# 32-bit attention products on 64 stationary columns, one query load per tile, and a new order

## The chip, the cores and the metric

The kernel runs on one core of a Trainium2 chip. The metric is the device time of one execution in microseconds (us), the median of several runs. TensorE (PE) multiplies, VectorE (DVE), ScalarE (ACT) and GpSimd (POOL) do the rest, and all DMAs are issued by SyncE (SP), whose queue is in order.

## The reference

Four batches of 768 positions go through an attention of eight heads (64 wide) and then a feed-forward layer of width 512 to 2048 to 512. A position attends to its window of 15 neighbours on both sides and to 24 block summaries (the maximum of 32 keys, the mean of 32 values):

```python
k_sum = k.reshape(B, H, nb, block, D).max(axis=3)
v_sum = v.reshape(B, H, nb, block, D).mean(axis=3)
scores_l = scale * np.matmul(q, k.transpose(0, 1, 3, 2))      # only |i - j| < 16 is kept
scores_s = scale * np.einsum('bhsd,bhnd->bhsn', q, k_sum) + np.log(block)
a = softmax(concatenate([masked scores_l, scores_s]))
x = np.matmul(a, np.concatenate([v, v_sum], axis=2))          # heads side by side: B x S x 512
xn = (x - mean) / sqrt(var + 1e-6) * g_ln
out = x + np.maximum(xn @ w_ch1, 0.0) @ w_ch2
```

## The kernel before

Positions are cut into 24 tiles T of 128, six per batch; two halves of four heads make 48 units t = 2T + hh.

**The first batch** (t = 0 to 11) is computed in 32 bits. `early_qk(t)` makes the scores: per unit two halves of the array's rows (`pr`, contraction over 64) and two heads (`v`), four matmuls with 128 stationary columns (the queries). `early_transp` transposes the probabilities against an identity (tiles `pp`), and `early_pv(t, pr)` multiplies them with the values into a tile `o`: one matmul of 128 columns on the common tail and two of 64 on the near values, again with 128 stationary columns, contraction over 128. In the first four units spare transposes of `ident` stand ahead of them.

**The other three batches** are computed with pairs of 16-bit numbers. `load_q` fetches queries into `qs` twice (one copy for each half of the partitions) and splits them, `heads(T)` makes scores and products with 64 stationary columns, the two halves of the output's partitions by turns, `late_softmax` follows. Before a batch starts, `batch(b)` passes its keys, queries and values through one staging tile (`bst`, one buffer) to find block sums and the largest magnitudes: each load is followed by an Abs with a sum on ACT, after which the next load may start. `batch_vput` writes the block means (`vsum`) into the value tiles by eight small DMAs per batch.

**The feed-forward layer** runs through all of it as the filling of PE. `g1(s)` makes a piece of the hidden layer (tile `h`, two buffers in PSUM), evicted by a Relu on ACT and a subtraction on DVE; `g2(s)` multiplies it into the outputs (tile `a`). Weights are merged, measured (`gram`) and split first.

**The order** on each engine is not that of the code. Every call is recorded in `Plan`, with a cost per instruction, and `Plan.issue` simulates all engines and writes the instructions out in the simulated order of their starts. The table `ORDER` shifts the rank of every step:

```python
early = 16.0 * np.frombuffer(base64.b85decode(ORDER), "<i4")
rank, best = [r + early[x.stage] for r, x in zip(rank, self.ops)], None
```

Each engine then runs its list strictly in order. A helper (line 356, after the change line 361) issues all of it, so the profile gives one line for everything and groups are told apart by tiles. DMA costs in `MOVE` are by partitions and bytes: time in the shared queue and tail; one number `ISSUE` or `TURN` is the issuing time on SP.

Of the kernel before, what the change touches and what calls it, by code (L numbers as in the profile page):

```python
# [34 lines left out]
NE = 192  # L35
# [24 lines left out]
    "nCAcgSgHU2Q#t?uV$A>l)BXSdK@<Q0=`;WU>qh_p4_E*I+0+03N8JDa9k>7g#GwEGn+X5_f13aQ$;to!&{O~bqq+b8UhV(?0doKVZ`l9;lm7qz"  # L60
    "Sk(Xj56S=k?JfWSl1cyowH5#X1^oa2e>wmF=EVR1?-"
    "u|7#@+w_(~<xG8w~&e1|t9fLr?$!W=jA7jcfn_5P1Lq5uE@3nLq#l=UM;&+}{8H9R&aYvj6}8v2p+azx@CIp#}f|WVrwTcA5YG=N|w7r=|b@Nk"
    "0Gp1ik<NJCy(bap3>|TCo5BUC#giIr;zpC6539A;JIusmTBTO%wnCpUwaO1q%QGS?T}(UI_pI!}kCGKh^*Ln;rlFxVHcQ>l6S0%@hCt)bIcQ5e"
    "EPOSqlIF`&s}1>0kf=1^EB}E4csvfS~{X+3ElPstN!A&C37(cjy2Ay^H_<$IAczzn%a8PMrV$Dq#Qs54`{XfY<;3?YsZ~jQ0Qkrv?B3IpF{QjO"
    "PFU$F2YW!T<mN;Kl#{xTydC6XpN^CK~_%!t?+CW8VM&m?QuIdKUlyG`;`-"
    "TgU(ZJ0t)ARZjo_R^k8u7^MII$F~3f>H`1(wkH4pD_j5ooCN>?CJq1q*NOlCI{E+q(!&4$JKF#MS<3(asmuTWix&U@^4S0XI<x=(c%=XTq80!E"
    "1dRXx_x1n(6<PoQ!1(|FlZ*fVR@(pnU>pDdArt@rJvsmY15^M2S3m#&(JBA{YbyW%3v2)YrYZmcWdZ;I1aJTVNiF~YKX?EDNBjT(2<`v>L|Xs="
    "Tp<7eHaP$QnX&)>;4c6G-a7yQX(a#v82|tOinIU!ZV><gB+dW-+@1gb9q<4Dz1{!+_DBE#EhPW|txNy_sLKEUKm-"
    "5)%&GtXdBp$!4!r;W8Uz3UBgFszR{#J1&gTFB@7(|YU=08OMz#O{PwM~w3L^jjyD<O&QWyXLEFJ&=&o2M~GHL(-#>oHw>|p=^B-"
    "a1`LgxSf=S2Vj1qlEEUjYCBAx;1Qdp-aFS{ncWU?%_o{0{&Cwm1L)2>t*6*2n+<#sB~REc*Zdvj6}9vp@g<Nk{+yjvD{~c-"  # L70
    "a5{Wf1@Xwr2nUur>eya!UXJUPk}`zHI;i>uvx50(t-djvD{~{!0J=Jsto6BtifH2U-9Cv`_#5w?+T}H6{Q6F+>0W7w-"
    "T6RyqIxI~o80flvSd&L02($}j)`e?0&I)c^nh3NHWvuo(aV+T{QL)baoSF24W&?=}DcIqm=d!twwA6S)8XGBp4I<6i&(vGM=^{^I}tQ1Ac$kk$"
    "YH1vmfzvcdoVRrde?$pQcX??C_naV!7;03QGV7100xg;M|k-"
    "v<By?JWQR1vCHvoX`LNnNI)!Qwab7c%T3OUG4w>L<Rr=(<%S}n9%?K3NruzoGbtUx=8>4U)=xyFaQ7mAHe_r*9-"
    "svyVw8!GNS+gDiZ(zDy{$j_ZI*FHv<3wzzP5Ww($S|T<ib;=)V8|BryO0OWXhdJ{SN1qVE6yMf?B%&msT-CqV!J2T1?`^-"
# [16 lines left out]
    "}!Kr;XUxhDVs-tYhak}d!M!@mFj3zPr<#JvCip&I}I16%+ADB1u29<u-cVUGX*6qEn|$5j9T!_@!(T)+SSVJiRttg8S2`1k++fx-"
    "X(Ru}*PCv^Y-L0<p>mMs7Ppwj>U94!C<A;SOvMyvn-Bs~BC88ZL?!NLFkyIcSO2Q&Zxeq8_ndKUlyD`)@!;#>d#K{5aU4jljhY#aapHB<lqv2g"
    "$Z=?nk>p+W!v$2b50HEsX^!%YAHekA|^rV;=EMF;=@<01e6Yb5{xo6i6LZ43YahB5#EpHct-"
    "4*387f<gcQaHaqM3&#Kdui^jyL0<p>dm{h<(7XTt73}~2AkqK-O1%I7RsjG2tS<lnAVvTHwe$b~eeD1Lk{<v7mZ|^$"
# [11 lines left out]
class Plan:  # L107
# [8 lines left out]
    MOVE = {
        "T": (1520.0, 550.0),
        (1, 2048): (170.0, 880.0),
        (128, 1024): (610.0, 490.0),
        (128, 1536): (680.0, 790.0),  # L120
        (128, 2048): (750.0, 880.0),
        (128, 2944): (1530.0, 960.0),
        (128, 3072): (1360.0, 1010.0),
        (128, 4096): (1770.0, 1290.0),
        (128, 576): (40.0, 2010.0),
        (24, 512): (110.0, 730.0),
        (32, 1024): (40.0, 820.0),
        (32, 2048): (40.0, 2000.0),
        (64, 1024): (220.0, 830.0),
        (64, 2048): (750.0, 770.0),  # L130
        (96, 1024): (490.0, 590.0),
        (96, 2048): (800.0, 700.0),
# [1036 lines left out]
```

## Time and profile before

| | |
|---|---|
| median of 2 runs | 632.82 us (631.36 to 634.27) |
| the profiled execution | 631.18 us, its span 629.4 us |
| PE busy | 616.1 us, 98% |
| DVE, ACT, POOL busy | 401.6, 351.1, 147.0 us |
| granted TensorE clock, mean | 0.995 |
| DMA | 89.52 MB, mean 142 GB/s |

A row of the page's groups reads: line, engine, operation, out<-in with shapes, count, then busy time and mean duration, then the idle time of the engine before it and what ended it. A row of a timeline begins with the start and the time that the row covers; ends of matmuls are modelled, so the pace of PE is read from starts. A row of stretches gives, for a stretch of time, its length and the busy time of PE, weight loads, DVE, ACT and POOL, then the granted clock, the DMA share and GB/s. One execution is profiled; sums are made against its own time.

### The profile page before, as it was taken

The numbers are of one execution on the slowest core, as the hardware profiler recorded it, in microseconds if no ns is written. First come the engines' busy times: TensorE is split into PE (matmuls) and PEld (weight loads), VectorE is DVE, ScalarE is ACT, GpSimd is POOL, SyncE is SP. The second block draws the span as 40 slices with busy tenths as digits, with TensorE's granted clock in tenths as the row PEclk, the third lists the DMA queues.
The fourth block names the chain that finished last, engine by engine and source line by source line (L and its number), as shares of the span: only waits on it lengthen the run. The fifth ranks groups of instructions, "written<-read, shape, count | busy, mean of one in ns | idle before, by whom it ended". The sixth has DMA issues, their size and how long they took to land.

```text
span 629.4 us, 14009 instructions
## 1 busy us (share of the span) xinstructions
PE 616.1 (98%) x5227; PEld 427.5 (68%) x5227; DVE 401.6 (64%) x1098; ACT 351.1 (56%) x926; POOL 147.0 (23%) x271
## 2 busy tenths in 40 slices
PE   8999999999999999999799999999999999999997
PEld 6777779885544676667377884577766756677754
DVE  4899999879668268846687465676877821171211
ACT  4898985459977257746677364565767711121100
POOL 4110302201333005403343022441433410030000
PEclk9999999999999999999799999999999999999999
DMA  9968798454797627555976426835776350011001
GB/s 285 308 175 259 237 302 231 99 159 120 192 226 166 151 73 191 155 159 134 199 209 139 95 70 125 188 83 146 176 152 151 74 120 0 1 48 23 1 25 43
DMA packets 115831, 89.52 MB, mean 142 GB/s; under 512 B 69553, under 2 KB 100273, under 8 KB 115762
## 3 DMA queue, kind: packets, MB, share of 16 engines
q1 hardware_dynamic: 115762, 88.61, 54.9%
q8 instruction: 41, 0.67, 0.4%
q14 instruction: 28, 0.23, 0.1%
HBM read 66.27 MB, written 6.29 MB: 115 GB/s over the span
## 4 chain that ended last, share of the span: by engine, by line
PE 60%; DMA 14%; ACT 10%; DVE 9%; SPq 4%; issue 2%; POOL 0%; ACTq 0%; DVEq 0%; POOLq 0%
PE h L356 26%; PE a L356 24%; SPq L356 4%; DMA bst<-in_ks 3%; DMA qs<-in_qt 3%; DMA bst<-in_vs 3%; PE o L356 3%; PE s L356 3%; DMA bst<-in_qa 2%; ACT p L356 2%; DVE m L356 2%; ACT bst L356 2%; PE low L356 1%; ACT w L356 1%; DVE kmax L356 1%
## 5 line engine op out<-in xcount | busy, mean ns | idle before, releaser
L356 PE MATMUL h<-xt,w_u 128*128 128x256 f16 x2304 | 264.5, 273 | 2.2 <-DVE h_x L356 2.2
L356 PEld LDWEIGHTS <-w_u 128*128 128x128 f16 x2304 | 224.8, 98 | 39.0 <-issue 5.0
L356 PE MATMUL a<-w,h_x 128*128 128x512 f16 (+1 forms) x960 | 211.8, 376 | 4.5 <-ACT h_x L356 4.1
L356 PEld LDWEIGHTS <-h_x 128*128 128x128 f16 x1008 | 98.0, 98 | 107.6 <-ACT h_x L356 5.1
L356 DVE SCALAR_TENSOR_TENSOR h_x<-h,h_x 128x512 f16<-128x512 f32 x80 | 54.1, 685 | 88.4 <-ACT h_x L356 88.3
L356 ACT ACTIVATE h_x<-h 128x512 f16<-128x512 f32 x80 | 46.2, 590 | 96.1 <-PE h L356 95.9
L356 ACT ACTIVATE p<-p,mn,sv 128x120 f32<-128x120 f32 x144 | 68.2, 475 | 12.6 <-POOL mn L356 12.3
L356 ACT ACTIVATE bst<-bst 128x384 f32<-128x384 f32 (+2 forms) x55 | 32.4, 589 | 52.3 <-DVE vsum L356 25.5
L356 POOL TENSOR_TENSOR p<-p,p 128x480 f16<-128x480 f32 x36 | 40.8, 1134 | 63.1 <-ACT p L356 52.4
L356 POOL TENSOR_TENSOR x<-x,rc 128x256 f32<-128x256 f32 x36 | 28.2, 789 | 94.5 <-DVE x L356 91.5
L356 PE MATMUL a<-w,h_y 128*128 128x512 f16 x192 | 43.6, 379 | 0.0
L356 POOL TENSOR_SCALAR mn<-mn,sv 128x4 f32<-128x4 f32 x36 | 19.2, 534 | 99.5 <-DVE mn L356 80.0
L356 DVE SCALAR_TENSOR_TENSOR m<-raw,m 128x512 uint32<-128x512 uint32 x64 | 42.1, 680 | 0.0
L356 DVE SCALAR_TENSOR_TENSOR qhl<-qs,sv,qhl 64x512 f16<-64x512 f32 x36 | 28.4, 788 | 18.9 <-ACT qhl L356 18.1
L356 DVE CUSTOM_DVE_ANT_0 p<-s,mask 128x120 f32<-128x120 f32 x144 | 33.4, 275 | 7.6 <-PE s L356 7.4
L356 ACT ACTIVATE qhl<-qs,sv 128x512 f16<-128x512 f32 x36 | 25.7, 714 | 19.8 <-DMA qs<-in_qt 14.8
L356 DVE SCALAR_TENSOR_TENSOR kl<-ksg,sv,kh 128x640 f16<-128x640 f32 x36 | 32.1, 891 | 7.3 <-ACT kh L356 6.9
L356 DVE SCALAR_TENSOR_TENSOR x<-a,scales,x 128x512 f32<-128x512 f32 (+1 forms) x24 | 17.7, 735 | 27.7 <-PE a L356 27.5
L356 ACT ACTIVATE kh<-ksg,sv 128x640 f16<-128x640 f32 x36 | 29.5, 821 | 6.9 <-DMA ksg<-in_kt 5.8
L356 PEld LDWEIGHTS <-h_y 128*128 128x128 f16 x192 | 18.7, 98 | 21.0
L356 DVE TENSOR_REDUCE x<-o 128x256 f32<-128x512 f32 x36 | 23.8, 684 | 9.1 <-PE o L356 9.1
L356 DVE SCALAR_TENSOR_TENSOR v<-vst,sv,v 128x512 f16<-128x512 f32 x36 | 29.2, 821 | 0.0
(116 smaller groups left out, 722.3 us busy)
## 6 DMA issues: line engine op xcount, KB each, us to landing
raw<-in_w SPq DMA_DIRECT2D x32, 512.0 KB
ksg<-in_kt SPq DMA_DIRECT2D x36, 368.0 KB
qs<-in_qt SPq DMA_DIRECT2D x72, 128.0 KB
out_x<-x SPq DMA_DIRECT2D x23, 256.0 KB
bst<-in_ks SPq DMA_DIRECT2D x20, 192.0 KB
bst<-in_qa SPq DMA_DIRECT2D x15, 256.0 KB
bst<-in_vs SPq DMA_DIRECT2D x20, 192.0 KB
vst<-in_va SPq DMA_DIRECT2D x36, 96.0 KB
```

Of the source, the lines that this page charges most:

```text
L356: getattr(getattr(nc, self.ops[i].engine), op)(*a, **k)
```

## The change

Four things change. In `early_qk` and `early_pv` each 32-bit matmul is issued twice, for the two halves `z` of the stationary columns, which write the two halves of the output's partitions. The planner's cost of such a half is half of the whole. The queries are loaded by one DMA that writes both halves. Issuing time in `MOVE` becomes a third number for each kind of DMA, all three numbers of every kind are new, and `ORDER` is a new table (its text is left out here).

```diff
-        "T": (1520.0, 550.0),
+        "T": (1320.0, 1450.0, 790.0),
...
-    ISSUE, TURN, BEGIN, TICK, SWITCH, FIRST = 470, 1250, 1100, 10240 / 3, 93, 3500
+    BEGIN, TICK, SWITCH, FIRST = 1100, 10240 / 3, 93, 3500
...
-        (128, 2048): (750.0, 880.0),
+        (128, 2048): (420.0, 850.0, 1060.0),
...
-        (24, 512): (110.0, 730.0),
+        (24, 512): (790.0, 100.0, 860.0),
...
-        for half in range(2):
-            nc.sync.dma_start(qs[D * half : D * half + D], qt[T, hh])
+        nc.sync.dma_start(qs[:], qt[T, hh].partition_broadcast(2))
...
-                    nc.tensor.matmul(ps[pr][:, v * NE : v * NE + w], q[:, v], k[:, v, :w], start=True, stop=True)
+                    for z in halves:
+                        nc.tensor.matmul(
+                            ps[pr][z, v * NE : v * NE + w], q[:, v, z], k[:, v, :w], start=True, stop=True
+                        )
...
-            nc.tensor.matmul(both, e[:, 1, :], tail, start=True, stop=False)
+            for z in halves:
+                nc.tensor.matmul(both[z], e[:, 1, z], tail, start=True, stop=False)
             for v in range(2):
                 j = 2 * v + pr
-                nc.tensor.matmul(ps[:, j, :], e[:, 2 * v, :], near[:, j], start=False, stop=v == 1)
+                for z in halves:
+                    nc.tensor.matmul(ps[z, j, :], e[:, 2 * v, z], near[:, j], start=False, stop=v == 1)
```

What the change moves is shown at three places. The first is PE early in the program, the PV products of unit 1 (tile `o_124`; `pT` are the transposed probabilities, `vst` and `spare_x` the values) and the scores of unit 4 (`s_..._160` and `161`). Before:

```order
L356 MATMUL s_0_160<-spare_x_100,spare_x_94 128x184
L356 MATMUL s_1_161<-spare_x_100,spare_x_94 128x184
L356 MATMUL s_0_160<-spare_x_100,spare_x_94 128x192
L356 MATMUL s_1_161<-spare_x_100,spare_x_94 128x192
L356 MATMUL o_124<-ident 128x128
L356 MATMUL o_124<-vst_77,pT_0_123 128x2x64
```

And now:

```order
L361 MATMUL o_124<-ident 128x128
L361 MATMUL o_124<-vst_77,pT_1_126 64x2x64 x2
L361 MATMUL o_124<-spare_x_96,pT_1_126 64x64 x4
L361 MATMUL s_0_160<-spare_x_100,spare_x_94 64x184 x2
L361 MATMUL s_1_161<-spare_x_100,spare_x_94 64x184 x2
L361 MATMUL s_0_160<-spare_x_100,spare_x_94 64x192 x2
L361 MATMUL s_1_161<-spare_x_100,spare_x_94 64x192 x2
L361 MATMUL pp_0_149<-ident,p_88 128x128 x3
```

Every row of the first batch's products stands for two matmuls on 64 partitions each, and the PV products no longer have the array shape of the transposes around them. Over the whole program PE's list has 12 runs of QK and 20 of the 64-column products of the later batches between full-array work before, and 12 of QK, 20 of the later batches and 21 of PV now. Four of the 21 border on a run of QK on one side; after 11 of them comes a 32-bit instruction of the full array.

The second place is ACT in the middle of the program, where queries of the fourth batch pass through `bst` (`bst92` and `bst93`, sums to `vabs3`) while tile 14 is attended to; `h38` and `h40` are hidden pieces with their Relu, `kh`, `qhl`, `v16` the split operands. Before:

```order
L356 ACTIVATE bst92_775,vabs3_761<-bst92_775 128x512
L356 ACTIVATE kh0_379<-ksg28_703,sv2_581 128x4x160
L356 ACTIVATE qhl28_702<-qs74_701,sv2_581 128x512
L356 ACTIVATE v16_0_378<-vst0_77,sv2_581 128x8x64
L356 ACTIVATE v16_1_382<-vst1_78,sv2_581 128x8x64
L356 ACTIVATE bst93_776,vabs3_761<-bst93_776 128x512
L356 ACTIVATE h38_x3_639<-h38_638 128x512
```

And now:

```order
L361 ACTIVATE h38_x3_639<-h38_638 128x512
L361 ACTIVATE bst91_774,vabs3_761<-bst91_774 128x512
L361 ACTIVATE h38_x3_639<-h39_640 128x512
L361 ACTIVATE p_87,sum26_684<-p_87,mn26_683,sv2_581 128x120 x3
L361 ACTIVATE p2_88,sum27_686<-p2_88,mn27_685,sv2_581 128x120
L361 CAST p16_376<-p_87 128x4x120
L361 ACTIVATE p2_88,sum27_686<-p2_88,mn27_685,sv2_581 128x120 x2
L361 ACTIVATE bst92_775,vabs3_761<-bst92_775 128x512
L361 ACTIVATE p2_88,sum27_686<-p2_88,mn27_685,sv2_581 128x120
L361 CAST p16_376<-p2_88 128x4x120
L361 ACTIVATE bst93_776,vabs3_761<-bst93_776 128x512
L361 ACTIVATE h40_x4_688<-h40_687 128x512
```

The Abs of `bst93` has moved from before the Relu of `h38` to before that of `h40`. On PE, 54 matmuls of `a` stand between the products of `h38` and those of `h40` now, and then the 24 of `h41`. On SP, in the same stretch, the loads of `bst92` and `bst93` now stand like this (`ksg` are keys, `pt` transposed probabilities; the last of the eight copies of `vsum2` stands 13 rows ahead of the first row, before the load of `bst89`):

```order
L361 DMA bst92_775<-in_qa 128x512
L361 DMA vst1_78<-in_va 64x256
L361 DMA qs77_724<-in_qt 128x1x512
L361 DMA vst1_78<-in_vb 32x256
L361 DMA vst1_78<-in_va 96x256
L361 DMA ksg30_726<-in_kt 128x2x368
L361 DMA_TRANSPOSE pt1_381<-p16_376 128x8x128
L361 DMA bst93_776<-in_qa 128x512
```

Before, six of the eight copies, two transposes and the two query loads stood between the two:

```order
L356 DMA bst92_775<-in_qa 128x512
L356 DMA qs74_701<-in_qt 64x512
L356 DMA vst0_77<-vsum2_569 24x128 x2
L356 DMA vst1_78<-vsum2_569 24x128
L356 DMA_TRANSPOSE pt0_377<-p16_376 128x8x128
L356 DMA vst1_78<-vsum2_569 24x128
L356 DMA qs74_701<-in_qt 64x512
L356 DMA vst1_78<-vsum2_569 24x128 x2
L356 DMA_TRANSPOSE pt0_377<-p16_376 128x8x128
L356 DMA bst93_776<-in_qa 128x512
```

The copies and the loads of this unit's queries have left the stretch between the two; loads of values and a transpose of the next tile stand there.

The third place is PE where the second batch's magnitudes are brought together (`vps1`). Before, products for the weights' size (`gram2`, of the merged weights `m2`) and of `h15` stand around it:

```order
L356 LDWEIGHTS m2_1_330
L356 MATMUL gram2_0_359<-m2_1_330 128x128
L356 MATMUL vps1_440<-ident_76,vm0_1_439 3x128
L356 LDWEIGHTS w1_u14_323
L356 MATMUL h15_412<-xt_1_186,w1_u14_323 128x256
```

And now products of `a0`:

```order
L361 LDWEIGHTS h0_y0_386
L361 MATMUL a0_1_388<-w2_3_363,h0_y0_386 128x512
L361 MATMUL vps1_440<-ident_76,vm0_1_439 3x128
L361 LDWEIGHTS h2_y1_391
L361 MATMUL a0_0_387<-w2_4_364,h2_y1_391 128x512
```

The output products of the first two tiles have moved ahead of the second batch's first scores; before, they began after them.

More of the change, by code (lines that the diff above doesn't have):

```diff
@@ L60 @@
[L60 to L75, printed above, removed]
@@ L92 @@
[L92 to L95, printed above, removed]
+    "QSJZ#i{t<QdmR7(uHgUw&#wRfvEBdw8@m7hbEN<O60QIL*{}cq$Or%c?%V(W4v_!<=-"
+    "2=M8TSAGExiB#Z?pgZ3q$|_Sr7mK@eBX}8;$?}KfnL~kJ|tLxm5rFG5Y`iSw#Q<y_x_28t4E2Z6E*u?5Y3%-"
@@ new lines @@
+    "k|^gx$yu04AcMrdX@kG<hlR<UHSk2`9S~xL>d49+r<C>thN9DU<CjGkJA7D^=SYA&Mg1{&msT-"
+    "2DJbGmWu!X;`#so4K@G(7|s9x2*&^a6P^G6;=lj@vi<-"
+    "6$EW}Q!N~vrJCXnY?3VxkBennk>5c#YfT;ifmD~USu8aTwp^N|jhPMCz*P;Lalmq|(UWWhw55)if`jP+tg5m%F4Tt~#ET{kf8IS+}n4kauYsLT"
+    "nyd(esaUK8w+Svd96Ab_W*T(<<CHnvW3XuQ*<In&9M)3dt`P2XZXx{(-"
+    "<mLbWqs0IJE$09Kg+TxSB+UQ+F}nZ%1RekYD{24$&JX|q^0fc|t;7HSag+c53>p9c0`UL;wlV+!y9EFMUm*Yh2}J+^C@ug1TH*iy@w)&2JfHvn"
+    "&Cvh<c=iAPMWp}#tLOj!L{0zzqo)7=2l4;^G+qDzg0uhsEjR!G!rTA<F5dtD{xbjo>1zN02Q&Zx02%-Q0cijL$0`5-"
@@ new lines @@
+    "sWJcn3j+WEhr<8=pD6$U;4uII%vk^c0$>0DeQW>#x>5iD)9?TPUt$0NGHU<;8p{9w_5=U`7zF?T)pP&=kR1R3h5P^iU&;Uf&$<8qtS<lnQ;h%r"
+    "|7-"
+    "vNbG85fT$2C)eCGfEJeB|ddZqvWNd5o+?uGyVf3pAoXW0M$wEqA9W(EKN7t#O!eB1y3t@r=`78L*h=;HtXqZ$AJ>$d;@;sO8wu<ZZ;&kq0qas&"
+    "VXpdSDL>2&}AYgPaNvEcvz?UVoip`ic&?eYKrSqcCEN3H+=;@<!Nf06(H6u|%gtiJ#M*^~eOa7zFH$kYG-BBB5P+pPcpuL}SGOcVeBgt7nsE7t"
+    "%2UXK6&vKIgVUDyBr%9{WGKJEYi4JZHrQUw42BLDyZmsS7(BVhmlLJt4{Iw}AFwkQAqb3Fh6kRt#9k^cYxE*}5@yA}Wd=2-"
+    "v$V{`xjn)3huLmmJCVW<E9(f0rUufYHRN)7-3pz;6z2-"
@@ new lines @@
+    "hr$cpU%$y&M1lI2!-"
+    "}HKqUmA4mWIbhQ8fwAcUtOS}L7v>E^a8bAO5Vh#WRRQ3P=ORWF@p}GJ6z#RYpS)Kp?W7+@zOz;2yAS?g?1s?zauk`=_Ou_&E;a30vt^xo6ickO"
+    "m?=AoUa>W1t^IHG_6%GIZIlBM<gWv!EW=8-3d{+PfjkEv%_3i)vnJWMQzB2#-"
+    "`H=trd(;2_9E|_}Gadi{W3&JN=ZpXUMiKx3^{)T_Qv(119rFMGw+a9Nkk9}B@YetT@X7!GzZw7l6Ndl)(J}x4rpW*Q<>UYVrWXJJH!J`Eax4G<"
+    "Y$*T$DFFZgV(<U|K|KHfIVk`D{{H{}0i*x_``G{g1e^c=&gB39JG1})4kiEqh35bN^ico+91;KkhD-ne(6s;mRZai^u$uq>^V<LatGNIF5|ID@"
+    "E|CBKmYV<nTd)8B=pFz7(!&4$kE;Lwr5OMKm&E`7S>ylz6SV*TQk?()9JBxb)z$z1Q>*{~opS&HZc+dM6W{;;xaI%<aH;?QJk|gIQbqs(Zqfh$"
@@ new lines @@
+    "54->Wys!WNr}6*))%O4Y)sp}JXdeIo(h&dv>Ei$YLIMB)UHt$5f-V36N#6heLHPgwdFlWE@CX0^y$t{Wo$>$waJc{fO_u-"
+    "v%SQkJu<HN+ez^bt0~Y`QHKqUm;wk_Dp49*Uwafqin!Nx2kFo#%5*`2mhK&FJd$9liE0h2KHlhFj6^;M@m6!kjm!JRtPMiP#cvS!Z3rPR~mbd@"
+    "^G?M@S=h6TFWsm>=b_oCgxwHTO^!@+;FTDT%gvI~=eF^{o$f*DS{IdW5NSXitOTz#E6mS3l6utldArAlmtGECEBZvS0FCG8@BGdo>3Gx5`N1gx"
+    "wyDb0!7_|TYfl~kg`t<+*aq|EFx5EGbRvrKVoV@@40*3$pNY4NN4#5BacnbgkP{9BH;0*u(1tI_d@Av=zDm(xHI-mdlfx`d)PtgDWx(EOO;=KR"
+    "=YV`mAo{#_kmL32ALs0+#W@rEaS91UWi(CKz11$gmit_*e91s8i0NelnSsVZWfX)B^VlMyyqU`_wNoD{5Ao>6Q^GyH%^2`7K3LpRgCQ|?a-"
@@ new lines @@
+    "%bDkQ$+v(*-"
+    "8Ka@$LWrmZ|^$tQi0RFxmhAOLhPNi}(NkYj*$u|4RS>NH+igU+@3_&@TW0h{FH>LF51bvj_kH2)6(K?==7b%`pG~rj7sq&MyD}xjO&=QD6W72+"
+    "aTgcl!VT#2o+tnq&X~yc_@k?OOl<Q!4-fl+^$KMP~p27%cz*MQ8v35ZV9#)5!n-"
+    "TD|}ONR|Kp5;On+8+QNzrt<&)?;rpGsR9510nq>d(6RsjY7+neXgUA@E;j%Gk+1*%#XJB2VDSI{bL9X355oWdo)Z87lqCQFRYU*)T~Yu5X8ZsD"
+    "Wa<C^ocRC$c;Wy5R~rBT^9cX|YE%FKBhvr>Em;5nHWUB=??M0ocwPVimpT9dJwyNiAxQuLWxD_W%(nmkaF_r8+8qD@ZIb{0@4o;40Ez$qMXmq;"
+    "Cb<9qc^?1(fjs~K6-NL7bVC3DWcvUA$Pxem;*tOVo)!QAWuE{45kCL`X1D+USg`;9TciK~43+=?vBLlVd0GGfU8n#5z}f%*`I-"
@@ new lines @@
+    "O!y{Z5Ibm;&83DW=n35Ngwh`Im&Z$<zBN}vD#B_99)4aEQdyNUn*0hRy%?uGyVFZ2KZJeB|doihLc&glRD6te&S4vGK&$}Io@k*ELv6%YUb-"
+    "%J1i;nDy9Rp|f!<O2WzA&LM0wV(h0t+N0B2)zIQi_8E22%i7{B<27Aa2o&s;@JQH?;rpGqKN<h%o+dy9_9c4s_Os$I*I@P_00eOyuJVbx8DE%<"
+    ";?&8Hmd*s))xQ(?;`*JO{o9>@3{Z}s3`ydez^bt^~nGKN3s9^<KzGT$)NxL`@{eL4buPrfdT*kB&q-"
+    "ZCNKa1BiaA|h0Oo|^~V4IFx>zDp4I>Vo#g-"
+    "j+8Y1>lAQnl&n^G}<;Va32Gjrlg|YwthR^^1nq&X~Js<!8#jXGUUXlO*mFxfi$YcNjL<ax>q0s;Tv1<STP^AC==OF+9`R4!s#R>obc5?s#o=gA"
+    "$C1C&nupR&a;WPjMG|T`08qfd#Bx(Qvom>C_Y1jY%wOarHO*8-"
@@ L96 @@
+    "i+DHHZdB*?$b7lYl)+Yb}nPmU~SpEP1!qET!cr5?`v|#`M_u&8kzFz<UT?GIDY-"
+    "j)gay0+|*a!dsF75ySa^nC0(Fy<nfJXoTz1RQ$+b{qC3I6~8gf;*Gz_|baO)UTb3W@*!S*rj4l)3-"
+    "^d>#M*hb;gAdZqvWw*UYCU)TTtJc<ARt@Qu@gD3z1s5}4w;=2F;&iDWSSPlRH!jk|0"
 )
@@ L113 @@
     SAME = dict(tensor=0, vector=127, scalar=143, gpsimd=100, sync=0)
-    ISSUE, TURN, BEGIN, TICK, SWITCH, FIRST = 470, 1250, 1100, 10240 / 3, 93, 3500
+    BEGIN, TICK, SWITCH, FIRST = 1100, 10240 / 3, 93, 3500
     FLIGHT = 8
     MOVE = {
-        "T": (1520.0, 550.0),
-        (1, 2048): (170.0, 880.0),
-        (128, 1024): (610.0, 490.0),
-        (128, 1536): (680.0, 790.0),
-        (128, 2048): (750.0, 880.0),
[L122 to L125, printed above, removed]
-        (24, 512): (110.0, 730.0),
[L127 to L132, printed above, removed]
+        "T": (1320.0, 1450.0, 790.0),
+        (1, 2048): (400.0, 100.0, 1030.0),
+        (128, 1024): (400.0, 560.0, 690.0),
+        (128, 1536): (400.0, 540.0, 1100.0),
+        (128, 2048): (420.0, 850.0, 1060.0),
+        (128, 2944): (460.0, 1570.0, 940.0),
+        (128, 3072): (450.0, 1360.0, 1210.0),
+        (128, 4096): (430.0, 1660.0, 1470.0),
+        (128, 576): (500.0, 40.0, 1900.0),
+        (24, 512): (790.0, 100.0, 860.0),
+        (32, 1024): (600.0, 40.0, 1040.0),
+        (32, 2048): (500.0, 40.0, 1430.0),
+        (64, 1024): (530.0, 360.0, 820.0),
+        (64, 2048): (545.0, 720.0, 920.0),
+        (96, 1024): (480.0, 460.0, 720.0),
+        (96, 2048): (410.0, 840.0, 780.0),
     }
@@ L209, in record @@
             columns = ({'matmul': 4, 'transpose': 2}[op] if ins[-1].dtype == F32 else 1) * math.prod(n for _, n in a[0].ap[1:]) * ins[0].ap[0][1] / P
+            columns /= 1 + (a[0].ap[0][1] == D and ins[-1].dtype == F32)
         if self.joined:
@@ L216, in record @@
         else:
-            half = engine == "tensor" and (3 if a[0].ap[0][1] == D else 1 if ins[0].ap[0][1] == P // 2 else 2 * (ins[-1].dtype in (F16, BF16)))
+            half = engine == "tensor" and (3 if a[0].ap[0][1] == D and ins[-1].dtype == F16 else 1 if ins[0].ap[0][1] == P // 2 else 2 * (ins[-1].dtype in (F16, BF16)))
             busy += 40 * (half == 3)
@@ L232, in cost @@
             if "transpose" in op:
-                return self.TURN, *self.MOVE["T"]
-            return self.ISSUE, *self.MOVE[x.ap[0][1], free(x) * size]
+                return self.MOVE["T"]
+            return self.MOVE[x.ap[0][1], free(x) * size]
         if engine == "tensor":
@@ L238, in cost @@
                 return 0.443 * max(n, 256) + 4.5, 0.0, 0.0
-            if a[0].ap[0][1] == D:
+            if a[0].ap[0][1] == D and dt == F16:
                 return max(n / 4.8 + 1.5, 14.0), 0.0, 0.0
```

28 lines of the change are left out of this document (6 added, 22 removed).

## The prediction

> **What bounds the kernel now.** I read the page's first two parts and its chain first, to see which engine the time belongs to.
>
> ```profile
> PE 616.1 (98%) x5227; PEld 427.5 (68%) x5227; DVE 401.6 (64%) x1098; ACT 351.1 (56%) x926; POOL 147.0 (23%) x271
> PE   8999999999999999999799999999999999999997
> PEclk9999999999999999999799999999999999999999
> PE 60%; DMA 14%; ACT 10%; DVE 9%; SPq 4%; issue 2%; POOL 0%; ACTq 0%; DVEq 0%; POOLq 0%
> ```
>
> TensorE (PE) is busy 98% of 629.4 us and the last product of the feed-forward layer ends the run. Work that leaves PE, or a wait that leaves PE, comes off the end nearly one for one; work on the other engines counts only where PE waits for it. One digit in both strips stands out, the twentieth slice (around 300 us). So the second view is PE's waits, the whole list:
>
> ```profile
> PE a L356 <- ACT h_x L356: 4.1, 2, 3.4
> PE h L356 <- DVE h_x L356: 2.2, 4, 1.2
> PE warm L356 <- POOL ident masks.py:199: 1.8, 1, 1.8
> PE vps L356 <- DVE vm L356: 0.8, 2, 0.6
> PE a L356 <- DVE h_x L356: 0.4, 1, 0.4
> PE v L356 <- DMA spare_x<-in_va: 0.4, 1, 0.4
> PE low L356 <- ACT w_u L356: 0.2, 1, 0.2
> ```
>
> Without the start (warm), PE waits 8.1 us in all, 3.4 of it at one place. There I look at PE and at ScalarE (ACT), in order of time, and at stretches of 5 us:
>
> ```profile
> 295.90 4.05 PE L356 MATMUL a<-w,h_x 128*128 128x512 f16 x18
> 303.38 1.03 PE L356 MATMUL a<-w,h_x 128*128 128x512 f16 x2 [3.43 <-ACT h_x L356]
> ...
> 297.71 1.32 ACT L356 ACTIVATE v<-vst,sv 128x512 f16<-128x512 f32 x2
> 302.12 0.63 ACT L356 ACTIVATE bst<-bst 128x512 f32<-128x512 f32 x1 [3.09 <-DMA bst<-in_qa]
> 302.75 0.58 ACT L356 ACTIVATE h_x<-h 128x512 f16<-128x512 f32 x1
> ...
> 300.00:305.00 5.00, 1.62 (x4) 0.53 (x5) 2.02 (x7) 2.03 (x4) 0.65 (x1) 0.75 1.09 239
> 305.00:310.00 5.00, 5.00 (x21) 2.67 (x20) 4.93 (x16) 4.86 (x15) 2.21 (x4) 0.56 0.59 165
> ```
>
> PE has run out of a-products: the next ones need a Relu, and the Relu stands on ACT behind an Abs whose data land at 302. The idle stretch then costs again: the granted clock is 0.75 and 0.56 in the two stretches, (1-0.75)x5 + (1-0.56)x5 = 3.45 us of lost clock. The place costs 3.43 + 3.45 = 6.9 us. Why the load was late stands in SP's queue:
>
> ```profile
> 286.16 1.61 SPq L356 DMA_DIRECT2D vst<-vsum  x2
> 289.51 2.29 SPq L356 DMA_DIRECT2D vst<-vsum  x3
> 293.25 0.74 SPq L356 DMA_DIRECT2D vst<-vsum  x1
> 294.67 1.74 SPq L356 DMA_DIRECT2D vst<-vsum  x2
> 297.87 0.53 SPq L356 DMA_DIRECT2D bst<-in_qa  x1
> L356 SPq DMA_DIRECT2D vst<-vsum x24: 713/732/1093, 118.4 to 428.5; - x24
> L356 SPq DMA_DIRECT2D qs<-in_qt x72: 471/479/1368, 109.1 to 486.3; - x72
> ```
>
> From 286 to 298 us SP does nothing but issue, 1.61 + 2.29 + 0.74 + 1.74 = 6.4 us of it for eight small copies of vsum at 0.73 us each. The old table of order costs priced every plain issue at 0.47 us; the new one prices this one at 0.79 and a transpose at 1.32.
>
> **Part 1, the first batch's QK products (12 units).** A 32-bit matmul is two pieces in the trace. A unit is 4 matmuls, 8 pieces, on two row halves of 64. Its row and PE's next:
>
> ```profile
> 42.13 0.56 PE L356 MATMUL o<-spare_x,pT 128*128 128x64 f32 x4
> 42.62 0.91 PE L356 MATMUL s<-spare_x,spare_x 64*128 64x184 f32 x8
> 43.45 0.72 PE L356 MATMUL h<-xt,w_u 128*128 128x256 f16 x5
> 26.54 0.39 PE L356 MATMUL o<-vst,pT 128*128 128x128 f32 x2
> 26.77 0.56 PE L356 MATMUL o<-spare_x,pT 128*128 128x64 f32 x4
> 27.16 0.28 PE L356 MATMUL o<-ident 128*128 128x128 f32 x1
> ```
>
> The unit takes 43.45 - 42.62 = 0.83 us. The first weight load is exposed (0.105, see part 2), the change of array shape behind it costs 0.10 (four o pieces take 27.16 - 26.77 = 0.39, yet s follows at 42.62, 0.49 after 42.13), so 0.63 us are streaming: four pieces of 0.16 per row half, both halves at once. With 64 columns there are 16 pieces on four quarters, still four per quarter; if the four run at once the stream stays 0.63 and only the exposed load halves: -0.05 x 12 = **-0.6 us**. Bounds: a load wholly hidden gives -1.3; column halves one after the other give 0.63 more, +7.0.
>
> **Part 2, the PV products (24 units).** From 26.54 to 27.16 six pieces take 0.62 us, 0.105 each whatever their length: the weight load of 128 columns sets the pace, not the 64 streamed columns (0.39 for four). 24 x 0.62 = 14.9 us. With halves, nothing of the kind is in the trace in 32 bits; the nearest rows are the later batches' 64-column units in 16 bits:
>
> ```profile
> 334.27 0.96 PE s L356 x32
> 335.23 0.70 PE o L356 x32
> 335.93 5.35 PE h L356 x48
> 334.96 0.22 PE L356 MATMUL s<-kh,qhl 128*64 128x120 f16 x2
> 335.01 0.22 PE L356 MATMUL s<-kl,qhl 128*64 128x120 f16 x2
> 335.07 0.86 PE L356 MATMUL o<-v,pt 128*64 128x128 f16 x32
> 335.86 0.50 PE L356 MATMUL h<-xt,w_u 128*128 128x256 f16 x3
> ```
>
> Two matmuls per 0.05 us, one on each half, where 120 streamed columns need 0.05 us by themselves (256 need 5.35/48 = 0.111 in the h row): the halves load and stream at once. I carry this over: per unit and half two pieces of 0.11 and four of 0.056, 0.444 us, loads of 64 columns (estimate 0.053, half of 0.105) hidden behind them. 24 x 0.444 = 10.7. But PV leaves the full shape. Each run of PV pays the change in and out, 0.10 + 0.10 as above (in the late unit h starts 0.79 after the first o at 335.07 where o streams 0.70), and an exposed load of 0.053: by the order there are 21 such runs, 21 x 0.25 = 5.3; four borders are shared with QK units, -0.4; in 11 of the 21 a 32-bit instruction comes next, whose own load of 0.105 is then exposed, +1.2. Sum 16.8 against 14.9: **+1.9 us**. Bounds: without the shape changes -4.2, which I exclude since no border in the trace goes free; halves one after the other, +10.7 more, +12.6.
>
> **Part 3, queries in one load.** 36 issues of 0.48 us go, 17 us from SP between 109 and 486 us. Bytes stay. SP is not what ends the run, so I credit nothing directly; it acts through part 4.
>
> **Part 4, the new order.** At the 300 us place the Abs of the same buffer (bst93) now stands before the Relu of h40, no longer before that of h38; PE has 54 a-products (4.05/18 = 0.22 each, 11.9 us) between h39's and h40's products, and h41's 24 after h40's before a product needs h40's Relu. On SP the eight vsum copies are past before the last five loads of that batch's queries. I take the whole 6.9 us: **-6.9**. Bounds: nothing goes, 0; or it goes with part of the rest. Second, between 100 and 150 us:
>
> ```profile
> PE h L356 <- DVE h_x L356: 1.8, 3, 1.2
> PE vps L356 <- DVE vm L356: 0.6, 1, 0.6
> ```
>
> PE had h and gram alone there, and waits 2.4 us for their evictions. Now the first a-products stand around vps1 and fill: I take **-1.5** (0 to -2.4). Third, an order of 9,769 rows drawn anew makes waits that the old one lacked. The other waits of the list sum to 8.1 - 3.4 - 2.4 = 2.3 us and I let them stand; for new ones I take **+2** (0 to +7, one more place like that at 300).
>
> **Sum** against the profiled execution's 631.2 us: -0.6 + 1.9 - 6.9 - 1.5 + 2 = -5.1, so 626.1. The median of the runs shown, 632.8, lies 1.6 above that execution, so the forecast for a median is **627.7 us**.
>
> **Rivals.**
> - *The waits only move* (part 4 gives nothing net): 632.8 + 1.3 = 634. For it: SP's queue is still in order and bst is one buffer. Against it: the pricing named above hits exactly the copies that made SP late.
> - *Column halves overlap only by turns.* If pieces of one row half start in the order of the program, the second half's first piece waits for the first half's second. PV then takes 0.11 x 3 + 0.056 x 4 = 0.554 per unit, +0.11 x 24 = 2.6; QK per row half five steps of 0.16 instead of four, +0.16 x 12 = 1.9: 632. If the row halves keep to that order too, a QK unit streams nine steps, 1.44 us instead of 0.63, +9.7: with PV's 2.6 the time is 640. For turns the trace speaks only by silence, since its 16-bit pairs alternate between the halves anyway. Against the harder form it has the QK row: five steps would be 0.80 us of streaming there, and it has 0.63. The Trainium skill, "TensorE: Matmul & The Clock Gate", section "Part 3: Packing small matmuls — row/col tiling", states that harder form: matmuls start and end strictly in program order, and a weight load overlaps a running matmul only in another row group. By that rule the time would be the 640; the trace disagrees for row halves, and no run here shows 32-bit column halves.
> - *Slower: a load lands late ahead of a Relu again.* bst93 now has six issues between it and bst92, one a transpose: about five of 0.5 and one of 1.3, 3.8 us, and the load then flies 4.2 us (issued at 297.87, its Abs at 302.12). If the load lands more than the 24 x 0.11 = 2.7 us of h41's products after h40's are done, PE stops, and a stop like that at 300 costs 6.9 us with the clock. Two batches after the first two pass their loads through that one buffer beside the late attention: one stop gives 627.7 - 2 + 6.9 = 632.6, the time of before; at both it is 639.5, slower than before.
> - *The halves do not act as halves* and run one after the other in 32 bits: +7.6 and +10.7 on the forecast, 646. The 16-bit pairs speak against it.
> - *All waits go and none comes:* 627.7 without the new 2.0, the 2.3 left standing and the last 0.9 of the stretch from 100 to 150: 622.5.
>
> **How the numbers follow.** Forecast 0.46 (625 to 631), waits only move 0.20, turns 0.13 (0.03 of it the harder form), late load 0.08, no overlap 0.05, all waits gone 0.08. The range reaches to 621, the last case less the 1.5 by which one run stands off a median, and to 637, waits that move with turns in part. It leaves out the late load, the harder form and no overlap, 0.16. A measurement of this kernel tells about 2% from no change: 620.2 and 645.5. Faster than that takes more than all the waits, 0.04; slower takes no overlap, 0.04; within, 0.92.
>
> **What would show it.** Part 1: a QK unit of about 0.78 us with 16 pieces in four quarters; 1.4 would be one half after the other. Part 2: PV pieces in pairs, about 0.25 us lost around each run; 24 units with borders near 17 us. Part 4: no PE wait over 1 us near 300 us, PEclk 9 in every slice after the start, PE's list of waits near 5 us instead of 8.1. Part 3: 36 qs loads. I am wrong if a wait of several us stands at another place with a dip of the clock behind it, or if 64 columns load no faster in 32 bits than 128, when PV stays at 0.1 per piece in each half and gains nothing against its borders.

## The result: slower by 15%, and the profile after

| | before | after |
|---|---|---|
| median of 2 runs | 632.82 us (631.36 to 634.27) | 729.87 us (728.64 to 731.1) |
| ratio | 1 | 1.1542 (95%: 1.1481 to 1.1602) |
| span of the profiled execution | 629.4 us | 729.3 us |
| granted clock, mean | 0.995 | 0.953 |

The forecast was 627.7 us and its range ended at 637. The page after the change, its busy times, two strips and the chain's shares by engine and by line:

```profile
PE 641.9 (88%) x5467; PEld 430.2 (59%) x5467; DVE 400.7 (55%) x1098; ACT 351.7 (48%) x926; POOL 148.8 (20%) x271
PE   8999999886697789688689779978799998999998
PEclk9999999998898999899899989998999999999999
DMA 38%; PE 32%; DVE 11%; ACT 10%; issue 5%; SPq 2%; POOL 1%; ACTq 0%; DVEq 0%; POOLq 0%
DMA qs<-in_qt 19%; PE h L361 13%; PE a L361 10%; DMA bst<-in_vs 5%; DMA bst<-in_qa 4%; ACT p L361 4%; DMA bst<-in_ks 3%; DVE qhl L361 2%; PE low L361 2%; PE o L361 2%; SPq L361 2%; PE s L361 2%; ACT qhl L361 1%; DVE x L361 1%; ACT bst L361 1%
```

DVE, ACT and POOL do the same work in the same time as before. What fell is PE's share, from 98% to 88%. Behind the start its strip is full up to the seventh slice (128 us) and has holes from there to near slice 29 (530 us): the stretch in which queries of the last three batches are loaded. In the chain DMA and PE have changed places (14% and 60% before), and one transfer, the queries' load, holds 19% of the span.

The list of waits, of after and then the same two waits of before (engine, tile, releaser: us in total, times, longest us):

```profile
ACT qhl L361 <- DMA qs<-in_qt: 107.6, 25, 6.0
DVE vsum L361 <- DMA bst<-in_vs: 40.6, 11, 8.2
```
```profile
ACT qhl L356 <- DMA qs<-in_qt: 14.8, 12, 3.5
DVE vsum L356 <- DMA bst<-in_vs: 13.6, 9, 5.6
```

ACT, at the split of the queries (`qhl`), waits 92.8 us more for their load than before. PE's own list says how that reaches the matmuls:

```profile
PE h L361 <- DVE h_x L361: 22.0, 10, 6.8
PE h L361 <- DMA xt<-x: 16.3, 4, 7.3
PE a L361 <- ACT h_x L361: 14.2, 3, 7.3
PE a L361 <- DVE x L361: 8.9, 4, 5.6
```

PE hardly names the queries (6.5 us in three waits for their split): it waits for evictions and Relus that stand on ACT and DVE behind the waiting split, and for tiles `xt`, whose DMAs are issued by SP in order. One place in full, by the timeline of ACT, SP and DVE:

```profile
188.91 0.56 SPq L361 DMA_DIRECT2D qs<-in_qt  x1
197.33 0.72 ACT L361 ACTIVATE qhl<-qs,sv 128x512 f16<-128x512 f32 x1 [5.36 <-DMA qs<-in_qt]
198.08 0.75 DVE L361 SCALAR_TENSOR_TENSOR qhl<-qs,sv,qhl 64x512 f16<-64x512 f32 x1 [5.86 <-ACT qhl L361]
198.87 0.52 SPq L361 DMA_DIRECT2D qs<-in_qt  x1
```

The load is issued at 188.91 and used at 197.33, 8.4 us later. ACT stands for 5.36 us of it and DVE for 5.86. The tile `qs` has one buffer, so the next load starts only when the split is done, at 198.87, one full flight per load. The stretch around it, after and then before (length; busy PE, weight loads, DVE, ACT, POOL; clock, DMA share, GB/s):

```profile
180.00:200.00 20.00, 13.34 (x112) 9.09 (x111) 6.40 (x23) 7.60 (x20) 0.50 (x2) 0.84 0.61 106
```
```profile
180.00:200.00 20.00, 20.00 (x151) 9.74 (x149) 14.31 (x43) 15.40 (x43) 9.43 (x13) 1.00 0.78 193
```

PE is idle for a third of the 20 us and the granted clock is 0.84 over them. Loads on the chain (start, us), first of after, then of before, where each is one of two half loads:

```profile
154.33 8.41 DMA qs<-in_qt
188.91 8.40 DMA qs<-in_qt
```
```profile
173.64 4.21 DMA qs<-in_qt
182.73 4.34 DMA qs<-in_qt
189.18 2.43 DMA qs<-in_qt
192.67 2.78 DMA qs<-in_qt
```

The transfer's 256 KB are what two half loads brought. It takes two to three and a half times as long as either. The records of single packets show how (start in us, ns, bytes; the first packets of 2048 bytes behind the issue at 188.91; those of 1472 bytes between them, of a load of keys, are left out):

```
191.464  84  2048
191.487  84  2048
191.544  84  2048
191.567  84  2048
```

There are two trains, each with one packet per 80 ns at first: 191.464, .544 and 191.487, .567. 128 packets of one row each make 64 per train, 64 x 0.080 = 5.1 us; the last one starts at 196.738, 5.3 us after the first.

### The profile page after: what moved, and what is told of

Same layout as the page of the kernel before. It is cut to its first block, busy times and chain, and to the rows that moved or that the text cites. A ratio compares the mean times of both kernels' runs of the same rounds, so it can differ in the third digit from the quotient of the medians.

```text
span 729.3 us, 14435 instructions
## 1 busy us (share of the span) xinstructions
PE 641.9 (88%) x5467; PEld 430.2 (59%) x5467; DVE 400.7 (55%) x1098; ACT 351.7 (48%) x926; POOL 148.8 (20%) x271
## 4 chain that ended last, share of the span: by engine, by line
DMA 38%; PE 32%; DVE 11%; ACT 10%; issue 5%; SPq 2%; POOL 1%; ACTq 0%; DVEq 0%; POOLq 0%
DMA qs<-in_qt 19%; PE h L361 13%; PE a L361 10%; DMA bst<-in_vs 5%; DMA bst<-in_qa 4%; ACT p L361 4%; DMA bst<-in_ks 3%; DVE qhl L361 2%; PE low L361 2%; PE o L361 2%; SPq L361 2%; PE s L361 2%; ACT qhl L361 1%; DVE x L361 1%; ACT bst L361 1%
## 5 line engine op out<-in xcount | busy, mean ns | idle before, releaser
L361 PE MATMUL h<-xt,w_u 128*128 128x256 f16 x2304 | 278.4, 281 | 39.2 <-DVE h_x L361 22.0
L361 PEld LDWEIGHTS <-w_u 128*128 128x128 f16 x2304 | 230.1, 101 | 85.5 <-issue 34.2
L361 PE MATMUL a<-w,h_x 128*128 128x512 f16 (+1 forms) x960 | 219.8, 384 | 23.7 <-ACT h_x L361 14.2
L361 ACT ACTIVATE qhl<-qs,sv 128x512 f16<-128x512 f32 x36 | 25.8, 717 | 107.6 <-DMA qs<-in_qt 107.6
L361 PE MATMUL a<-w,h_y 128*128 128x512 f16 x192 | 46.7, 397 | 8.0 <-DVE qhl L361 3.7
L361 POOL TENSOR_TENSOR x<-x,rc 128x256 f32<-128x256 f32 x36 | 26.2, 738 | 74.8 <-DVE x L361 74.2
L361 DVE TENSOR_REDUCE vsum<-bst 96x16 f32<-96x512 f32 x20 | 13.6, 678 | 40.6 <-DMA bst<-in_vs 40.6
L361 DVE SCALAR_TENSOR_TENSOR x<-xn,rs,x 128x512 f16<-128x512 f32 x24 | 18.9, 787 | 24.5 <-ACT x L361 24.4
```

The costliest lines, as they stand in the source:

```text
L361: getattr(getattr(nc, self.ops[i].engine), op)(*a, **k)
```

## The experiments

Theory A: the broadcast load is slow by itself, because its source has the two copies as its outermost dimension and so two trains of packets. Rivals: B, the new order makes the waits; C, the 64-column halves cost more than the sum had; D, any single load of both halves into the one buffer is bad, whatever its source. The expectations call A, B and C theories 1, 2 and 3. In all kernels below the instructions of every engine stand in the same order as in the kernel that each starts from, but for the edit itself. A ratio is that to the kernel before, measured on the same chip in the same rounds; its 95% interval stands in brackets.

**Everything but the broadcast.** The change with the old two half loads at the place of the one; the planned cost of the pair is that of the one, so that the order stays.

```diff
-        (64, 2048): (545.0, 720.0, 920.0),
+        (64, 2048): (210.0, 850.0, 1060.0),
...
-        nc.sync.dma_start(qs[:], qt[T, hh].partition_broadcast(2))
+        with pl.unit():
+            for half in range(2):
+                nc.sync.dma_start(qs[D * half : D * half + D], qt[T, hh])
```

> The changed kernel with the queries loaded by two DMAs again, one per half of the partitions, at the place of the one; every engine's order is otherwise the same. Theory 1 (the broadcast load is slow in itself: its 128 packets run in two trains, on two of the 16 DMA engines, about 8.3 us from issue to use instead of 2.5 to 4.5): 622 to 640 us. Theory 2 (the new order is slow whatever the load): 700 us or more. Theory 3 (the 64-column halves in 32 bits are slow): 700 us or more.

Measured: 625.53 us (622.18 to 626.53, 4 runs), ratio 0.9886 [0.9844, 0.9928]. Its page, then its waits:

```profile
PE 613.2 (98%) x5467; PEld 422.1 (68%) x5467; DVE 402.3 (64%) x1098; ACT 353.1 (57%) x926; POOL 154.2 (25%) x271
PEclk9999999999999999999999999999999999999999
ACT qhl L361 <- DMA qs<-in_qt: 8.6, 10, 1.5
PE h L361 <- DVE h_x L361: 2.5, 3, 1.0
PE gram L361 <- DVE scales L361: 1.7, 2, 1.2
PE a L361 <- ACT h_x L361: 0.8, 1, 0.8
```

One line takes the 15% away and leaves a kernel a little faster than before. B and C fall as causes of the loss. The profiled spans split it: 729.3 - 624.5 = 104.8 us, of which PE's busy time is 641.9 - 613.2 = 28.7 (the same 5,467 matmuls, at a mean clock of 0.953 against 1.0) and its idle time the other 76.1.

**The broadcast alone.** The kernel before, with its own order and 128-column products; the first half load becomes the broadcast and the second is left out. This is done where `Plan.issue` writes the instructions out, so that the plan has the two loads as before and the order stays: `whole` replaces the arguments of a call, and an empty one leaves the call out.

```diff
+            whole = getattr(self.ops[i], "whole", None)
             for op, a, k in self.ops[i].calls:
+                if whole is not None:
+                    if not whole:
+                        continue
+                    a = whole
...
             nc.sync.dma_start(qs[D * half : D * half + D], qt[T, hh])
+            pl.ops[-1].whole = (qs[:], qt[T, hh].partition_broadcast(2)) if half == 0 else ()
```

> The kernel before with the one broadcast load at the place of the first of its two loads, the second left out; all else as before. Theory 1: slower by 60 to 110 us, 690 to 740 us. Theories 2 and 3: 630 to 636 us.

Measured: 736.22 us (735.4 to 737.27, 4 runs), ratio 1.1647 [1.161, 1.1685].

```profile
PE 645.8 (88%) x5227; PEld 439.5 (60%) x5227; DVE 400.5 (55%) x1098; ACT 351.2 (48%) x926; POOL 145.5 (20%) x271
ACT qhl L361 <- DMA qs<-in_qt: 54.8, 16, 8.6
ACT kh L361 <- DMA ksg<-in_kt: 37.0, 12, 6.2
DVE vsum L361 <- DMA bst<-in_vs: 46.0, 13, 7.4
142.83 8.19 DMA qs<-in_qt
```

The load is as slow here (8.19 us on the chain) and costs 104 us in an order that was not drawn for it, as much as in the new one (729.87 - 625.53 = 104). ACT's own wait for the queries grows by only 40 us here (54.8 against 14.8); the waits for keys (37.0 against 5.8) and for values in `bst` (46.0 against 13.6) grow as well, so the slow load also holds up others.

**One load, but of rows that lie in memory.** The queries are laid out twice by the host's layout step, which only copies; the load then reads 128 rows in a row.

```diff
-        nc.sync.dma_start(qs[:], qt[T, hh].partition_broadcast(2))
+        nc.sync.dma_start(qs[:], qt[T, hh])
...
+    qT = np.concatenate([qT, qT], axis=2)
```

> The changed kernel with one load of 128 different rows: the queries lie twice in memory, as the keys already do, so that the DMA repeats nothing. Order the same. Theory 1: 620 to 636 us, and a load lands in about 3 to 4 us. If one large DMA instead of two is the cause, not the repetition: 700 us or more. Theories 2 and 3: 700 us or more.

Measured: 621.55 us (620.07 to 622.83, 4 runs), ratio 0.9833 [0.9792, 0.9874]. Waits, the stretch of above, and the issues of these loads (us each, least, median, most), here and then in the kernel after:

```profile
ACT qhl L361 <- DMA qs<-in_qt: 2.6, 4, 0.9
180.00:200.00 20.00, 20.00 (x218) 11.64 (x217) 16.24 (x48) 16.25 (x43) 9.55 (x12) 1.00 0.73 178
L361 SPq DMA_DIRECT2D qs<-in_qt x36: 323/347/530, 119.1 to 486.1; - x36
```
```profile
L361 SPq DMA_DIRECT2D qs<-in_qt x36: 521/576/607, 120.6 to 592.7; - x36
```

D falls: a single load of the same bytes into the same buffer is the fastest so far. The packet records no longer form two trains: the last packet of the load issued at 171.66 starts at 173.96, 2.3 us after the issue, where above it was 7.8 us. Its issue takes 0.35 us where the broadcast takes 0.58.

**The order without the halves.** As in the first experiment, with both products on 128 columns again (`early_qk` and `early_pv` as before, one matmul where the change has two).

> As the changed kernel with two loads, and the first batch's products on 128 stationary columns again; order the same. Theory 1: within 1% of the kernel with two loads; by the sum of the prediction (-0.6 and +1.9 us for the halves) 1.3 us faster than it. Theory 3: faster than it by tens of us. Theory 2: 700 us or more, like it.

Measured: 626.37 us (621.49 to 627.99, 4 runs), ratio 0.9896 [0.9845, 0.9946]. The order alone brings 632.26 - 626.37 = 5.9 us; the halves on top of it, 0.8 us with ranges that overlap.

**How many groups.** 128 distinct rows in memory, nothing broadcast, but in N groups with an unused row behind each, so that the source's outermost dimension has N entries. The lines for N = 2 are shown; for 4 and 16 only the sizes change (33 and 32, 9 and 8 in place of 65 and 64). N = 2 has the broadcast's two groups without its repeated reads.

```diff
-        nc.sync.dma_start(qs[:], qt[T, hh].partition_broadcast(2))
+        src = qt[T, hh]
+        nc.sync.dma_start(qs.rearrange("p j l -> p (j l)"), bass.AP(src.tensor, src.offset, [[65 * DM, 2], [DM, 64], [1, DM]]))
...
+    rows = np.concatenate([qT, qT], axis=2).reshape(TT, 2, 2, 64, DM)
+    qT = np.zeros((TT, 2, 2, 65, DM), np.float32)
+    qT[:, :, :, :64] = rows
```

N = 2:

> The changed kernel, its query load reading 128 different rows that lie in two groups of 64 with an unused row behind each group: the outermost dimension of the source has two members, as in the broadcast, and nothing is read twice. Theory 1a (a load runs on as many DMA engines as the outermost dimension has members): as the changed kernel, 715 to 745 us, loads of 8 to 9 us in two trains. Theory 1b (reading the same rows twice is what is slow): 618 to 626 us, like the load without repetition.

N = 4:

> The same with four groups of 32 rows. Theory 1a: four trains of 32 packets at 0.080 us, 2.6 us instead of 5.1, so loads about 2.5 us shorter than with two groups, near 5.7 us, and a time between the two, 635 to 680 us. Theory 1b: 618 to 626 us. If any grouping of rows costs the same: 715 to 745 us.

N = 16:

> The same with sixteen groups of 8 rows. Theory 1a: all 16 engines, 618 to 627 us, loads of 3 to 4 us, like the plain load of 128 rows. Theory 1b: the same 618 to 626 us. If any grouping of rows costs the same: 715 to 745 us.

| groups | time, us (2 runs each) | ratio | ACT's wait for qs, us | issue to use, median us | packets per group x 0.080 us |
|---|---|---|---|---|---|
| broadcast (2) | 729.87 | 1.1542 [1.1481, 1.1602] | 107.6 | 8.3 | 5.1 |
| 2 | 728.59 | 1.1548 [1.1525, 1.1571] | 106.4 | 8.3 | 5.1 |
| 4 | 667.56 | 1.0581 [1.0559, 1.0602] | 61.3 | 6.3 | 2.6 |
| 16 | 624.78 | 0.9903 [0.9869, 0.9936] | 5.9 | 3.7 | 0.64 |

The fifth column is the median from issue to the split, over those loads that ACT waited for, worked out from the trace. For each kernel the wait and a load on the chain, N = 2, 4 and 16:

```profile
ACT qhl L361 <- DMA qs<-in_qt: 106.4, 25, 6.0
152.70 8.23 DMA qs<-in_qt
```
```profile
ACT qhl L361 <- DMA qs<-in_qt: 61.3, 23, 4.2
148.94 6.37 DMA qs<-in_qt
```
```profile
ACT qhl L361 <- DMA qs<-in_qt: 5.9, 9, 2.0
174.26 3.43 DMA qs<-in_qt
```

Two groups of distinct rows cost what the broadcast costs, so reading a row twice is not the cause; the number of groups is. With 4 groups the records show four trains at the same pace (152.091, .100, .105, .118, then 152.171, .180, .185, .198). From 2 to 4 groups the flight falls by 2.0 us and the packets of a group by 2.5; from 4 to 16, by 2.6 and 2.0. A flight is thus 3.1 to 3.7 us (8.3 - 5.1, 6.3 - 2.6, 3.7 - 0.64 give 3.2, 3.7, 3.1) and one group's packets one after the other. With 4 groups a load is 0.6 us longer than the 5.7 expected: behind the issue at 148.94 the 128 packets of 2 KB start between 150.43 and 154.19, over 3.8 us and not 2.6, as the four trains do not begin together.

**The better load in the old order.** The kernel before with queries twice in memory and one plain load, put in where the instructions are written out, by the same lines on `whole` as above.

```diff
-            nc.sync.dma_start(qs[D * half : D * half + D], qt[T, hh])
+            nc.sync.dma_start(qs[D * half : D * half + D], qt[T, hh, :D])
+            pl.ops[-1].whole = (qs[:], qt[T, hh]) if half == 0 else ()
...
+    qT = np.concatenate([qT, qT], axis=2)
```

> The kernel before, its order kept, with one plain load of 128 rows (queries twice in memory) at the place of the first of its two loads. If what the new order gains (626 against 632 us with two loads) and what a plain single load gains (621 against 626 us in the new order) are two separate things: 626 to 630 us, with the wait at 300 us still there. If the single load by itself removes the wait at 300 us, because SP's queue comes forward: 618 to 624 us. If SP's queue does not matter in the old order: 630 to 634 us.

Measured: 625.82 us (624.4 to 630.74, 10 runs), ratio 0.993 [0.9903, 0.9958]. The stretch at 300 us that the prediction looked at:

```profile
300.00:305.00 5.00, 4.40 (x26) 2.12 (x23) 4.94 (x15) 5.00 (x16) 2.27 (x4) 1.00 0.56 151
```

PE has 4.40 us of 5 there where it had 1.62, at full clock, and PE's longest wait for a Relu in the whole run is 0.5 us (3.4 before). So the wait at 300 us goes without a new order, as the second expectation had it, yet the time lies at the edge of the first one's. The plain load's gain (630.73 - 625.82 = 4.9 us) and that of the order (5.9) nearly add: both together, with whole products, bring 10.1 (631.19 - 621.12, the run "both whole" below). The runs do not separate how much of the 4.9 comes from SP's 36 issues less.

**Each half alone.** On the version with plain loads: both products in halves again, both whole, only the scores (QK) in halves, only PV in halves.

```diff
-                    for z in halves:
-                        nc.tensor.matmul(
-                            ps[pr][z, v * NE : v * NE + w], q[:, v, z], k[:, v, :w], start=True, stop=True
-                        )
+                    nc.tensor.matmul(ps[pr][:, v * NE : v * NE + w], q[:, v], k[:, v, :w], start=True, stop=True)
...
-            for z in halves:
-                nc.tensor.matmul(both[z], e[:, 1, z], tail, start=True, stop=False)
+            nc.tensor.matmul(both, e[:, 1, :], tail, start=True, stop=False)
...
-                for z in halves:
-                    nc.tensor.matmul(ps[z, j, :], e[:, 2 * v, z], near[:, j], start=False, stop=v == 1)
+                nc.tensor.matmul(ps[:, j, :], e[:, 2 * v, :], near[:, j], start=False, stop=v == 1)
```

Both in halves:

> The changed kernel with the plain load of 128 rows once more, with both products in halves, as the base for the three beside it: 620 to 623 us. QK units 0.905 us from the end of what is ahead to the next full-array work, PV units 0.70 to 0.80, as read from the trace with two loads.

Both whole (the whole diff):

> As the base, both products on 128 stationary columns. If the halves cost what the prediction's sum says (QK -0.6, PV +1.9) and PE has no waits to absorb it: 1.3 us faster than the base. If PE's waits absorb it or the order was fitted to the halves: within 1 us or slower.

Scores in halves (the diff's second and third piece):

> As the base, QK in halves and PV on 128 columns. By the sum the fastest of the four, 1.9 us below the base.

PV in halves (its first piece):

> As the base, PV in halves and QK on 128 columns. By the sum the slowest of the four, 0.5 us above the base.

| | time, us | ratio |
|---|---|---|
| both in halves | 620.42 (620.04 to 620.44, 4 runs) | 0.9834 [0.9811, 0.9857] |
| both whole | 621.12 (618.54 to 621.79, 5) | 0.9835 [0.9807, 0.9863] |
| QK in halves | 619.74 (618.56 to 620.62, 4) | 0.9823 [0.9797, 0.9849] |
| PV in halves | 620.62 (620.05 to 621.52, 4) | 0.9839 [0.9815, 0.9864] |

The four lie within 1.4 us and their intervals overlap. The measurement doesn't separate the halves' effect from nothing; what can be said is that it is of the size of 1 us or less. In the trace of the base a QK unit takes 0.80 us to the next work and loses 0.09 at the border ahead of it, 0.89 where 0.905 was expected; a PV unit 0.60 and 0.09, just under the 0.70 to 0.80. All four beat both kernels by more than their intervals reach: the version with the plain load is the one to keep, at about 620 us, 1.7% under the time before.

## Why the prediction was wrong

**Part 3 is the step that failed.** It counted the issues that go and the bytes that stay, and took the flight of a load as unchanged, without a bound for it. The merged load was an operation that the trace of before did not show: its source had another shape. From its issue to the split it takes 8.3 us (median of the 25 splits that waited for it) where the second half load took 3.2 (of 12). Over 36 loads that would be some 180 us more (36 x 5.1); ACT waits 92.8 us more for the queries, and the time grows by 97. The Trainium skill has a rule for such a source, in "DMA: Bandwidth & Descriptors", section "Rules for kernel authors": an outermost dimension of size c below 16, such as a leading broadcast of c copies with stride zero, confines a transfer to at most c DMA engines. That rule spoke against this change, and the prediction did not draw on it. The runs agree with it as far as they show it: two trains with 2 groups, four with 4, and the load of 16 groups about as quick as the plain one (3.7 and 3.8 us from issue to use). The packet records name no engine. What it costs here is some 80 ns per packet of 2 KB, one after the other in each group.

The prediction's sentence that SP doesn't end the run held, but the conclusion was too short. The nothing that part 3 credited stood for two things: the slow flight, +104 us, and what one plain load brings against two half loads, -4.0 us in the new order and -4.9 in the old one. A load's issue is SP's; its flight belongs to whoever waits for the data, here ACT. With one buffer and queues in order, 5 us of flight become, as at 188.91, 5 us of ACT and DVE, then a late Relu, then an idle PE and a lower clock. That is the very path of the 300 us place, read there and not carried over to the 36 loads.

None of the rivals' times was near. The late-load rival had the right kind of stop, data that land late ahead of a Relu and then a lower clock, but for `bst`, at two places at most, 639.5 us. The case of no overlap, 646, rested on column halves. For the part that did the harm there was no rival at all. What did come true is the prediction's own sign of being wrong, waits of several us with a dip of the clock behind them.

**Part 4 came out near its number.** With half loads instead of the broadcast the changed kernel takes 625.5 us, 2.2 under the forecast. The order alone brought 5.9 us where the sum had 6.4, two numbers closer than the runs can tell. PE's waits were to come to near 5 us: in the first experiment they come to 7.8 with 1.8 of the start, 6.0 without, the longest 1.2, and the clock's strip is 9 in every slice. Near 300 us PE stood 0.79 us for a Relu, at full clock, instead of 3.43. Two things in this part were off. The clock's loss at 300 us was put at 3.45 us over the whole 10 us, but PE was idle for part of it; stretches of 1 us show 0.50 from the restart at 303.38 to 309 and 0.82 in the next, so 5.62 x 0.50 + 0.18 = 3.0, and the place cost 6.4. And most of that place goes with one plain load in the old order too, so the new order is not the only thing that removes it.

**Parts 1 and 2** hold in the trace, while their net effect is too small for the times. PE's timeline in the first experiment, a QK unit and a PV unit:

```profile
87.17 0.60 PE L361 MATMUL h<-xt,w_u 128*128 128x256 f16 x4
87.70 0.87 PE L361 MATMUL s<-spare_x,spare_x 64*64 64x184 f32 x16
88.50 1.16 PE L361 MATMUL h<-xt,w_u 128*128 128x256 f16 x9
49.78 0.71 PE L361 MATMUL h<-xt,w_u 128*128 128x256 f16 x5
50.42 0.44 PE L361 MATMUL o<-vst,pT 128*64 128x128 f32 x4
50.69 0.40 PE L361 MATMUL o<-spare_x,pT 128*64 128x64 f32 x8
51.02 0.83 PE L361 MATMUL h<-xt,w_u 128*128 128x256 f16 x6
```

The QK unit takes 88.50 - 87.70 = 0.80 us with its 16 pieces in four quarters (0.83 before, 0.78 forecast), and so do ten more of the twelve. The PV unit takes 51.02 - 50.42 = 0.60 from its first piece to the next work, and about 0.09 at the border ahead of it, 0.69 as against the sum's 0.444 + 0.25. So the four quarters do run at once, and the rivals of turns and of no overlap are out. The Trainium skill ("TensorE: Matmul & The Clock Gate", "Part 3: Packing small matmuls — row/col tiling") states that matmuls start and end strictly in program order. From that rule the prediction had worked out nine steps of 0.16 us, 1.44 us, for the scores of a unit; they take 0.80 with all that is around them. The trace has the first pieces of the four quarters 7 ns apart, but it does not tell in what order the two pieces of each matmul stand in the program. So it shows that the nine steps are wrong; whether the rule is, or the reading of it, stays open.

**The other loads.** ACT and DVE also wait longer for other loads after the change (`vsum` for `bst`, 40.6 us against 13.6). One such load on the chain, issued 2.26 us behind the query load of 198.87:

```profile
201.13 8.34 DMA bst<-in_qa
```

The packet records show why, behind the load of 188.91. A load of keys (packets of 1472 bytes) was issued at 189.83 and one of `bst` (2048 bytes) at 191.05. Most of their packets had started by 194.1; from there the records hold little but the two trains. When these end, at 196.8, 32 packets of 1472 bytes follow until 197.74 and 16 of 2048 until 198.4, of either load two sixteenths: these packets stood behind the trains. Over the whole trace, loads of `bst` and `ksg` issued less than 6 us after a query load took 6.9 us to land (median of the 17 that an engine waited for), the others 3.3 (of 15); with two half loads both are 3.5.

**What stays open.** How the 97 us divide between ACT's wait for the queries and the loads held up behind them is not separated; in the old order the waits for those others grow by more in sum than the wait for the queries. The net effect of the halves lies below what the times can tell.

## What to carry to other kernels

A merged DMA is priced by its own flight, not by issues saved and bytes kept: look at the source's outermost dimension first, and let it be the 128 partitions. To have small data twice on the chip, lay them out twice in memory and load them plainly, rather than repeat them with a leading dimension of two. Where a tile has one buffer and its reader sits in an ordered queue, much of a longer flight becomes that engine's wait (92.8 us here), and what waits behind it is found by asking who is queued there.
